# The first layer of a third batch in block form, and q and k loaded in the order that the transposes read

## The chip, the core and the metric

One core of one Trainium2 chip. TensorE multiplies matrices and writes to PSUM. VectorE (DVE in the profile) and ScalarE (ACT) read PSUM and work elementwise. GpSimd (POOL) issues the loads that turn f32 into bf16 on the way, and SyncE (SP) issues the DMA transposes and the stores. The metric is the device time of one execution in microseconds, as a median over runs.

## The reference

```python
# q, k, v: (8, 12, 448, 64)   w_in: (768, 2048)   w_out: (2048, 768), all f32
scores = scale * np.matmul(q, k.transpose(0, 1, 3, 2))
attn = np.maximum(scores, 0.0) ** 2 / S
attn_out = np.matmul(attn, v)
x = attn_out.transpose(0, 2, 1, 3).reshape(B * S, H * D)      # (3584, 768)
h = x @ w_in
g = 0.5 * h * (1.0 + erf(h * inv_sqrt2))
out = g @ w_out                                               # (3584, 768)
```

So each of eight batches has twelve heads of attention with a squared relu in place of the softmax, and all 3584 rows then go through two layers with an exact Gelu between them.

## The kernel before

**Attention.** Heads are taken four at a time (three groups g per batch, G = 3), and the 448 keys in seven steps i of 64. A step (`add_steps`, L610) is four score matmuls on quarters of TensorE's array into one of three two-bank PSUM buffers `w` (L623), then a relu on ScalarE or VectorE (L635, L637), then a square on VectorE (L644). After the seven steps of a group comes AV (`add_av`, L683: 28 matmuls, also into a `w` buffer), and two copies bring its result to `xT`, the transposed x of the batch.

**First layer.** In the plain form (`add_f1`, L730) a batch is 16 chunks m of 128 columns of w_in, each six matmuls of 448 columns, followed by one Gelu on ScalarE (L740). In the block form (`add_blocks`, L811, and `add_block`, L859) w_in and x are each cut into 2 x 2 blocks and multiplied with seven block products p1 to p7 in place of eight; sums of w_in blocks (`add_wsums`, L794), sums of x blocks (`xs`, L837) and five additions per quarter (v2, v3, c22, c21, c12, L904) make up for the eighth. The order of products is p1, p6, p2, p7, p5, p4, p3, each for two halves y; matmuls there have 224 columns (L870). Batches 6 and 7 have this form, and all others the plain one.

**Second layer.** Rows are taken in groups of 256 (`add_group`, L1000), and each group is seven products of eight matmuls of 384 columns (L1036), with four sums on VectorE ahead (L1017) and seven passes out of PSUM (L1070 and copies). Group 0 is made plainly (`add_plain`, L1131). The activations `h_sb` are a ring of two batches.

**Loads.** For batches 3 to 7, `add_load` (L446) issues three DMAs on GpSimd: k into `nk`, q into `nq` and v into `v_sb`. When they have landed, VectorE copies k and q into the tiles `pk` and `pq` in another order of columns (`add_pk`, L466, three copies a batch; `add_pq`, L477, six). SyncE then issues three transposes kT<-pk and four qT<-pq (`add_T_dma`, L569, L578), and a small copy on GpSimd (`add_gate`, L590) waits for those of qT: GpSimd works through its queue in order, so the loads of the next batch stand behind this gate. The first score step of a batch needs all four qT transposes of it. `nq`, `nk`, `pq` and `pk` exist once; qT and kT twice; v three times.

**What sets the order.** A planner in the program (`Scheduler`, L110) places every operation on an engine by estimated times. For the first 270 operations the order is a list written out by hand (`ORDER`). From then on TensorE's order is a list, `pe_q`: each batch b from 2 to 7 has six slots of attention steps, with first-layer chunks and second-layer products from one list `flow` between them, in equal shares per batch; `LEADS` puts some of them ahead of a batch. After attention, the list `end` follows: block batches with four products of a group woven in, and the remaining groups. VectorE and ScalarE choose by deadlines (`deadlines`, L206), which are worked out backwards from when TensorE needs each result. SyncE's transposes are ordered with the stores by the same deadlines. The plan is made twice (`PASSES`), and the last plan is used.

Of the kernel before, what the change touches and what calls it, by code (L numbers as in the profile page):

```python
# [49 lines left out]
PASS_BIAS = -0.4  # L50
SUM_BIAS = -0.3
TSUM_BIAS = 0.2
LEADS = {3: 8}
LAST = 256
PASSES = 2
NEAR = 0.5
QUEUE_STEP = 1.5
LOAD_MARGIN = 2.0


def cols(half):
# [41 lines left out]
class Scheduler:  # L103
# [39 lines left out]
    def pick(self, ops, only=None):  # L143
        top, near = None, []
        for n, op in enumerate(ops):
            t = self.ready(op)
            if t is None:
                continue
            for x, (eng, dur, lat) in enumerate(op.engines):
                if self.late and only not in (None, eng):  # L150
                    continue
                est = max(t, self.free[eng])
                if isinstance(lat, tuple):
                    est = max(est, self.landed[-8])
                if eng == "PE" and op.mode != self.mode:
                    est += SWITCH
                key = (est + op.bias + x * op.other, n)
                if top is None or key < top[0]:
                    top = (key, est, op, eng, dur, lat)
                near.append((est + x * op.other, est, n, op, eng, dur, lat))  # L160
        if top and self.late and only in ("ACT", "DVE"):
            edge = min(near)[0] + NEAR
            top = min(
                ((self.late[id(o)], n), est, o, eng, dur, lat)
                for at, est, n, o, eng, dur, lat in near if at <= edge
            )
        return top
# [26 lines left out]
    def run(self, fixed):  # L194


        for _ in range(PASSES):
            self.reset()
            self.place(fixed)
            self.deadlines()  # L200
        self.open = []
        n = len(ORDER.split())
        for est, op, eng in self.log[:n] + sorted(self.log[n:], key=lambda x: x[0]):
            op.fn(eng)

    def deadlines(self):  # L206


        after = {id(o): [] for o in self.open}
        for o in self.open:  # L210
            for d in o.deps:
                if id(d) in after:
                    after[id(d)].append(o)
                elif isinstance(getattr(d, "op", None), Op):
                    after[id(d.op)].append(o)
        takers = {}
        for _, o, _ in self.log:
            for name in o.need:
                takers.setdefault(name, []).append(o)
        for name, v in self.given.items():  # L220
            n = self.buffers[name]
            for x, o in enumerate(v):
                if x + n < len(takers[name]):
                    for y in [o] + list(o.joint):
                        after[id(y)].append(takers[name][x + n])
        self.late = {}
        t = math.inf
        order = sorted(self.log, key=lambda x: x[0])
        pe = [o for _, o, e in order if e == "PE"]
        ideal, at = {}, 0.0  # L230
        for o in pe:
            ideal[id(o)] = at
            at += o.engines[0][1]
        shift = pe[-1].start - ideal[id(pe[-1])]
        queue = math.inf
        for est, o, e in reversed(order):
            t = ideal[id(o)] + shift if e == "PE" else est + 50.0
            if e == "SP" and o.mode == "X":
                t = min(t, queue - QUEUE_STEP)
            for s in after[id(o)]:  # L240
                if id(s) in self.late:
                    t = min(t, self.late[id(s)] - (o.done - o.start))
            if e == "SP" and o.mode == "X":
                queue = t
            self.late[id(o)] = t
# [38 lines left out]
def kernel(  # L284
# [151 lines left out]
    def add_v(b, g0, g1):  # L436
# [6 lines left out]
        for g in range(g0, g1):  # L443
            ld_v[b, g] = [o]

    def add_load(b, g0=0, g1=G):  # L446
        add_k(b, g0, g1)
        add_q(b, g0, g1)
        add_v(b, g0, g1)
# [219 lines left out]
    def add_av(blk, bias):  # L669
# [31 lines left out]

        def get_x():
            if b not in xT:
                xT[b] = xpool.tile([128, HP, S], BF16, tag="xT", name="xT")
            return xT[b][:, 2 * g : 2 * g + 2, cols(half)]

        old = [o for (bb, *_), o in F1.items() if bb == b - 2]
        xs = X[b, g, half] = []
        for j in range(2):
            xs.append(  # L710
# [54 lines left out]
    def wtile(n, m):  # L765

        if n == 3:
            return wpart(0, 1), m
        if n not in wsum:
            tags = {1: ("nq",), 2: ("pq",), 4: ("nk", "pk")}[n]  # L770
            wsum[n] = [
                natpool.tile([128, K1, FF // 2 // len(tags)], BF16, tag=t, name=f"ws{n}")
                for t in tags
            ]
        k = M1 // len(wsum[n])
        return wsum[n][m // k], m % k
# [7 lines left out]
    def add_wsums(after, done):  # L784

        last = [o for (bb, *_), o in list(Pq.items()) + list(Pk.items()) if bb == B - 1]
        last += [o[0] for (bb, *_), o in list(Tq.items()) + list(Tk.items()) if bb == B - 1]
        add, sub = mybir.AluOpType.add, mybir.AluOpType.subtract

        def one(n, m0, op, a, b, deps):  # L790
            m1 = m0 + M1 // 2
            return sch.add(
                (("DVE", 0.95, 1.07),),
                lambda e: V.tensor_tensor(wcols(n, m0, m1), a(m0, m1), b(m0, m1), op=op),  # L794
                deps + last + after,
            )

        def part(i, j):
            return lambda m0, m1: wpart(i, j, m0, m1)

        def summed(n):
            return lambda m0, m1: wcols(n, m0, m1)

        for m0 in (0, M1 // 2):
            s1 = one(1, m0, add, part(0, 1), part(1, 1), [])
            s2 = one(2, m0, sub, summed(1), part(0, 0), [s1])
            s4 = one(4, m0, sub, part(1, 0), summed(2), [s2])
            s3 = one(3, m0, sub, part(0, 0), part(0, 1), [s1] + done)
            WS[m0] = {1: s1, 2: s2, 3: s3, 4: s4}

    def add_blocks(b):  # L811
# [10 lines left out]
        def t(n):  # L822
            def fn():
                if "t" not in box:
                    tag = {B - 2: "qT", B - 1: "kT"}[b]
                    box["t"] = tpool.tile([128, 4, K1, HS], BF16, tag=tag, name="xs")
                return box["t"][:, n - 1]

            return fn

        gone = old_T(b + 2 if b == B - 2 else b + 1)
        gone = [o for (bb, *_), o in QK.items() if bb == B - 2]

        def xsum(n, op, l, r, deps):
            return sch.add(
# [23 lines left out]
    def add_block(b, m4, y, ms, bank, x, t, TS, xs, old, half):  # L859
# [39 lines left out]
        def passed(name, to, other, deps, need=()):  # L899
            def fn(e):  # L900
                if other is None:
                    copy(e, get(to), ps(name))
                else:
                    V.tensor_add(get(to), ps(name), get(other))  # L904

            eng = e_copy(S, 1)
            return sch.add(eng if other is None else eng[:1], fn, deps, need=need, bias=PASS_BIAS)

        def gelu(src, r, c, deps, frees=()):
            def fn(e):  # L910
# [376 lines left out]
    def at(b, n):  # L1287
        return [at_slot(b, n)]

    add_load(3)  # L1290
    flow, plans = [], {}
    F1B = {2: 1, 3: 2, 4: 3, 5: 4, 6: 5}
    GROUPS = {2: (1,), 3: (2, 3), 4: (4, 5), 5: (6,), 6: (7, 8)}
    for b in range(2, B):
        add_steps(steps(b), dve=True)
        if b == 2:
# [7 lines left out]
        if b + 1 < B:  # L1304

            n = {2: 2, 3: 2}.get(b, 1)
            add_pk(b + 1, 0, G, after=at(b, n) + SUMS[0] + SUMS[1])
            add_pq(b + 1, 0, G, after=at(b, n) + SUMS[0] + SUMS[1])
            add_T_dma(b + 1, [at(b, n + (y >= 4)) for y in range(7)])
            if b + 2 < B:  # L1310
                add_gate(b + 1)
                add_load(b + 2)
        flow += [y for g in GROUPS.get(b, ()) for y in add_group(g)]
    add_wsums(at(B - 1, 1), [F1[B - 3, m, None] for m in range(KF)])

    def woven(x, y, n):


        tx, ty, gone, out = sum(o[0] for o in x), sum(o[0] for o in y[:n]), 0.0, []
        k = 0  # L1320
        for o in x:
            out.append(o)
            gone += o[0]
            while k < n and (k + 0.5) / n < gone / tx:
                out.append(y[k])
                k += 1
        return out + y[k:]

    end = woven(add_blocks(B - 2), add_group(9), 4)
    g10 = add_group(10)  # L1330
    end += g10 + woven(add_blocks(B - 1), add_group(11), 4)
    end += add_group(12) + add_group(13)
    pe_q.extend(x[1] for x in first_atoms)
    share, gone, edge = sum(x[0] for x in flow) / (B - 2), 0.0, 0.0

    def take():
        w, o = flow.pop(0)
# [3 lines left out]
    for b in range(2, B):  # L1341
        for _ in range(LEADS.get(b, 0)):
            gone += take()
        start, edge = gone, edge + share
        for n, slot in enumerate(plan[b]):
            for kind, x in slot:
                if kind == "FFN":
# [37 lines left out]
```

## Time and profile before

| what | value |
|---|---|
| median of 3 runs | 376.32 us (376.17 to 376.45) |
| the profiled execution, own time | 375.98 us |
| its span in the profile | 374.2 us |
| attention of batch 2 starts, attention of batch 7 ends | 65.3 us, 290.2 us |
| score matmuls of batches 3, 4, 5, 6, 7 start | 113.1, 140.1, 177.4, 214.6, 251.5 us |
| last matmul starts | in the group from 368.3 us |

Some groups of instructions, as the page counts them over the whole span: busy time, mean of one, and idle time of the engine just before them.

```profile
L635 ACT ACTIVATE a_sq<-ps 128x896 bf16<-128x896 f32 (+1 forms) x143 | 122.8, 914 | 57.5 <-PE ps L623 57.5
...
L644 DVE TENSOR_TENSOR a_sq<-a_sq 128x896 bf16<-128x896 bf16 (+1 forms) x169 | 98.7, 615 | 11.2 <-ACT a_sq L635 10.1
...
L904 DVE TENSOR_TENSOR part<-pb,part 128x448 f32<-128x448 f32 x40 | 23.1, 618 | 6.3 <-PE pb L870 6.2
...
L590 POOL COPY gate<-qT 128x4 bf16<-128x4 bf16 x5 | 1.3, 266 | 155.6 <-DMA qT<-pq 155.6
```

A line names the source line, the engine, the output and input tiles with their shapes, and the count. In the last one GpSimd sits idle for 155.6 us before the five gates: this is where it waits for the transposes.

### The profile page before, as it was taken

What the parts mean: (1) busy time and instruction counts of PE and PEld (TensorE: products, weight loads), DVE (VectorE), ACT (ScalarE), POOL (GpSimd) and SP (SyncE); (2) the same over time, 40 slices, a digit from 0 to 9 for tenths busy, and PEclk for the clock granted to TensorE, in tenths of its full rate; (3) what the DMA queues carried; (4) which work ended last, traced back from release to release, by engine and by line L of the source; (5) the groups of instructions that cost most, each with busy time, mean ns of one, the idle gap of its engine ahead of it and who ended that gap; (6) DMA issues with size and microseconds to landing.
All of it is one profiled execution on the core that took longest, in us unless ns stands there. A gap on an engine that the chain in (4) does not pass through costs nothing.

```text
span 374.2 us, 8324 instructions
## 1 busy us (share of the span) xinstructions
PE 363.0 (97%) x3485; PEld 215.4 (58%) x3485; DVE 284.3 (76%) x517; ACT 200.9 (54%) x301; POOL 46.0 (12%) x69
## 2 busy tenths in 40 slices
PE   8799999999999999999999999999999999999995
PEld 7566645455554455544555445544555886688663
DVE  3998981799848787985889768946888879785762
ACT  4998864746337865666546575657562333035100
POOL 8666400300002011002000020000000000000000
PEclk9999999999999999999999999999999999999999
DMA  9999999997579969989333799400020201210233
GB/s 175 195 201 204 202 190 114 171 205 143 94 171 162 146 75 190 238 113 159 64 101 79 140 154 181 120 3 0 2 86 12 75 2 31 90 49 2 85 86 84
DMA packets 69685, 42.96 MB, mean 115 GB/s; under 512 B 37776, under 2 KB 66192, under 8 KB 69648
## 3 DMA queue, kind: packets, MB, share of 16 engines
q0 software_dynamic: 30512, 22.47, 40.2%
q1 hardware_dynamic: 38768, 19.46, 25.5%
q8 instruction: 27, 0.44, 0.5%
q10 hardware_dynamic: 368, 0.51, 0.4%
q14 instruction: 10, 0.08, 0.1%
HBM read 45.61 MB, written 11.01 MB: 151 GB/s over the span
## 4 chain that ended last, share of the span: by engine, by line
PE 84%; DVE 6%; ACT 4%; issue 2%; DMA 2%; POOL 1%; DVEq 0%; ACTq 0%; POOLq 0%
PE pso L1036 32%; PE psh L730 29%; PE ps L623 8%; PE pb L870 7%; PE pav L683 4%; ACT a_sq L635 4%; PE pso L1131 3%; DVE a_sq L644 3%; DVE part L904 2%; DMA nk<-in_k_dram 2%; DVE a_sq L637 1%; DVE xT L387 0%; DVE kT L387 0%; PE tp L517 0%; ACT xT L389 0%
## 5 line engine op out<-in xcount | busy, mean ns | idle before, releaser
L635 ACT ACTIVATE a_sq<-ps 128x896 bf16<-128x896 f32 (+1 forms) x143 | 122.8, 914 | 57.5 <-PE ps L623 57.5
L730 PE MATMUL psh<-xT,win_sb 128*128 128x448 bf16 (+1 forms) x612 | 114.2, 342 | 0.1
L644 DVE TENSOR_TENSOR a_sq<-a_sq 128x896 bf16<-128x896 bf16 (+1 forms) x169 | 98.7, 615 | 11.2 <-ACT a_sq L635 10.1
L730 PEld LDWEIGHTS <-win_sb 128*128 128x128 bf16 x612 | 57.4, 98 | 53.7 <-issue 9.2
L740 ACT ACTIVATE h_sb<-psh 128x448 bf16<-128x448 f32 x96 | 52.5, 547 | 34.3 <-PE psh L730 34.0
L1036 PEld LDWEIGHTS <-s_sb 128*128 128x128 bf16 x424 | 40.6, 98 | 27.7 <-issue 2.5
L623 PE MATMUL ps<-qT,kT 64*64 64x448 bf16 (+1 forms) x756 | 48.5, 336 | 3.1 <-ACT a_sq L635 0.7
L637 DVE TENSOR_SCALAR a_sq<-ps 128x896 bf16<-128x896 f32 x26 | 28.2, 1088 | 28.5 <-PE ps L623 28.1
L1036 PEld LDWEIGHTS <-h_sb 128*128 128x128 bf16 x312 | 29.8, 98 | 20.9 <-issue 2.4
L1036 PE MATMUL pso<-wout_sb,h_sb 128*128 128x384 bf16 x208 | 38.1, 326 | 0.0
L1036 PE MATMUL pso<-t_sb,s_sb 128*128 128x384 bf16 x208 | 38.1, 326 | 0.0
L1036 PE MATMUL pso<-wout_sb,s_sb 128*128 128x384 bf16 (+2 forms) x216 | 38.1, 320 | 0.0
L683 PE MATMUL pav<-a_sq,v_sb 64*64 64x448 bf16 (+1 forms) x756 | 36.8, 330 | 0.8 <-ACT a_sq L635 0.4
L623 PEld LDWEIGHTS <-kT 64*64 64x64 bf16 x756 | 18.6, 105 | 26.9 <-issue 21.3
L1070 DVE TENSOR_TENSOR osb<-pso,p_sb 128x384 f32<-128x384 f32 x39 | 21.6, 555 | 9.5 <-PE pso L1036 7.3
L683 PEld LDWEIGHTS <-v_sb 64*64 64x64 bf16 x756 | 21.1, 107 | 13.1 <-issue 2.3
L387 DVE CAST xT<-pav 128x448 bf16<-128x448 f32 (+1 forms) x44 | 24.3, 582 | 5.5 <-PE pav L683 4.9
L904 DVE TENSOR_TENSOR part<-pb,part 128x448 f32<-128x448 f32 x40 | 23.1, 618 | 6.3 <-PE pb L870 6.2
L913 ACT ACTIVATE h_sb<-part 128x448 bf16<-128x448 f32 x24 | 13.3, 577 | 18.4 <-DVE part L904 18.3
L590 POOL COPY gate<-qT 128x4 bf16<-128x4 bf16 x5 | 1.3, 266 | 155.6 <-DMA qT<-pq 155.6
L870 PEld LDWEIGHTS <-win_sb 128*128 128x128 bf16 x192 | 18.4, 98 | 3.2 <-issue 2.1
L1036 PE MATMUL pso<-t_sb,h_sb 128*128 128x384 bf16 x104 | 19.0, 326 | 0.0
(60 smaller groups left out, 262.1 us busy)
## 6 DMA issues: line engine op xcount, KB each, us to landing
nk<-in_k_dram POOLq DMA_DIRECT2D x5, 672.0 KB, 6.7
nq<-in_q_dram POOLq DMA_DIRECT2D x5, 672.0 KB, 9.3
v_sb<-in_v_dram POOLq DMA_DIRECT2D x5, 672.0 KB, 13.4
out_dram<-osb SPq DMA_DIRECT2D x8, 336.0 KB, 3.1
wout_sb<-in_moe_w_out_dram POOLq DMA_DIRECT2D x2, 1152.0 KB, 11.7
v_sb<-in_v_dram POOLq DMA_DIRECT2D x9, 224.0 KB, 9.0
out_dram<-osb SPq DMA_DIRECT2D x7, 288.0 KB, 3.1
out_dram<-osb SPq DMA_DIRECT2D x8, 240.0 KB, 2.8
```

Source lines behind the costliest of these rows:

```text
L387: V.tensor_copy(dst, src)
L623: nc.tensor.matmul(ps[64 * j : 64 * j + 64, e, x * w : x * w + w], kT[r, g, i * 128 + 64 * j : i * 128 + 64 * j + 64], qT[r, 2 * g + j, co ...
L635: A.activation(ar, ps, AF.Relu, scale=c_att)
L637: V.tensor_scalar(ar, ps, c_att, 0.0, op0=mybir.AluOpType.mult, op1=mybir.AluOpType.max,)
L644: V.tensor_mul(box["a2"][:, :, :used], ar, ar)
L683: nc.tensor.matmul(pav[0][o2 : o2 + 64, e, :w], vt[b][r, 2 * g + e, bass.ts(i, D)], box["a2"][r, e, o : o + w], start=(i == 0), stop=(i == ...
L730: nc.tensor.matmul(ph[:, x * n : x * n + n], win_sb[:, kd, bass.ts(m + x, 128)], xT[b][:, kd, c], start=(kd == 0), stop=(kd == KD - 1),)
L740: A.activation(h_ring()[:, m : m + nm, o + c.start : o + c.stop], box[0][:, :S].rearrange("p (x n) -> p x n", x=nm), AF.Gelu,)
L870: nc.tensor.matmul(bank[name][:, y, z * HS : z * HS + HS], w[:, k, bass.ts(mm, 128)], right()[:, k], start=first and k == 0 and z == 0, st ...
L904: V.tensor_add(get(to), ps(name), get(other))
L1036: nc.tensor.matmul(box[bank][:, n0:n1], left()[:, kf], right[:, kf, n0:n1], start=bool(need) and kf == 0, stop=kf == K2 - 1, skip_group_ch ...
L1070: V.tensor_add(out()[:, n0:n1], box[bank][:, n0:n1], other()[:, n0:n1])
```

## The change

Batch 5 (B - 3) takes the block form as well, behind attention: `end` becomes blocks of 5 with group 7, group 8, blocks of 6 with group 9, group 10, blocks of 7 with group 11, and groups 12 and 13. The tiles `xT` of batches 5 to 7 and two of the w_in sums move to pools that are free by then. In the weave, a group's product now stands after the fourth and the tenth of each fourteen block products. The block form's first copy out of PSUM (v1) is made by ScalarE alone.

For batches 3 to 7, k and q are loaded straight into `pk` and `pq` in the permuted order, with runs of 64 elements, by 6 and 12 DMAs; the VectorE copies of these batches go. The planner's deadlines for TensorE now come from its operations one after the other without waits; it makes five plans and takes the one that ends first; and it may ignore the preference for ScalarE where ScalarE would be late.

```diff
-LEADS = {3: 8}
+LEADS = {3: 4}
+SHARES = (1.3, 1.0, 1.0, 1.0, 1.0, 1.0)
-PASSES = 2
+PASSES = 5
+LIMIT = 0.1
+QUEUE_MARGIN = 5.0
+WIDE = 2.0
...
-                near.append((est + x * op.other, est, n, op, eng, dur, lat))
+                other = op.other
+                if x and self.late:
+                    first = max(t, self.free[op.engines[0][0]]) + op.engines[0][2]
+                    if first > self.limit[id(op)] + LIMIT:
+                        other = 0.0
+                near.append((est + x * other, est, n, op, eng, dur, lat))
...
+        best = None
         for _ in range(PASSES):
             self.reset()
             self.place(fixed)
             self.deadlines()
-        self.open = []
+            end = self.free["PE"]
+            if best is None or end < best[0]:
+                best = (end, list(self.log))
+        self.open, self.log = [], best[1]
...
             ideal[id(o)] = at
-            at += o.engines[0][1]
-        shift = pe[-1].start - ideal[id(pe[-1])]
+            at = o.start + o.engines[0][1]
...
-                    t = min(t, self.late[id(s)] - (o.done - o.start))
+                    m = QUEUE_MARGIN if e == "SP" and o.mode == "X" else 0.0
+                    t = min(t, self.late[id(s)] - (o.done - o.start) - m)
+            self.limit[id(o)] = t + (o.done - o.start)
...
+    def add_wide(b):
+        def k_fn(e):
+            def fn():
+                to = get_p()[1].rearrange("p g (i e d) -> e p g i d", e=2, d=D)
+                src = kv_view(k, b, 0, G).rearrange("p (g e) (i d) -> e p g i d", e=2, d=D)
+                for g in range(G):
+                    nc.gpsimd.dma_start(to[e][:, g], src[e][:, g])
+            return fn
+        def q_fn(e, j):
+            def fn():
+                to = get_p()[0].rearrange("p c (g j e d) -> j e g p c d", j=2, e=2, d=D)
+                src = q[b].rearrange("(g e j) (p c) d -> j e g p c d", e=2, j=2, c=NC)
+                for g in range(G):
+                    nc.gpsimd.dma_start(to[j][e][g], src[j][e][g])
+            return fn
...
+        ks = [dma(k_fn(e), WIDE * n / 2, war(b), G) for e in range(2)]
+        qs = [dma(q_fn(e, j), WIDE * n / 4, war(b), G) for e in range(2) for j in range(2)]
...
     def add_load(b, g0=0, g1=G):
+        if b > 2:
+            return add_wide(b)
...
-            tags = {1: ("nq",), 2: ("pq",), 4: ("nk", "pk")}[n]
+            tags = {1: ("nq",), 2: ("pq",), 4: ("xT", "pk")}[n]
...
-            return sch.add(eng if other is None else eng[:1], fn, deps, need=need, bias=PASS_BIAS)
+            return sch.add(eng[1:] if other is None else eng[:1], fn, deps, need=need, bias=PASS_BIAS)
...
-    F1B = {2: 1, 3: 2, 4: 3, 5: 4, 6: 5}
-    GROUPS = {2: (1,), 3: (2, 3), 4: (4, 5), 5: (6,), 6: (7, 8)}
+    F1B = {2: 1, 3: 2, 4: 3, 5: 4}
+    GROUPS = {2: (1,), 3: (2, 3), 4: (4, 5), 5: (6,)}
...
-            add_pk(b + 1, 0, G, after=at(b, n) + SUMS[0] + SUMS[1])
-            add_pq(b + 1, 0, G, after=at(b, n) + SUMS[0] + SUMS[1])
...
+    def woven(x, y):
+        out, y = [], list(y)
+        for n, o in enumerate(x):
             out.append(o)
+            if n % 14 in (3, 9):
+                out.append(y.pop(0))
+        return out + y
+
+    end = woven(add_blocks(B - 3), add_group(7))
+    end += add_group(8)
+    end += woven(add_blocks(B - 2), add_group(9))
     g10 = add_group(10)
-    end += g10 + woven(add_blocks(B - 1), add_group(11), 4)
+    end += g10 + woven(add_blocks(B - 1), add_group(11))
     end += add_group(12) + add_group(13)
...
-        start, edge = gone, edge + share
+        start, edge = gone, edge + total * SHARES[b - 2] / sum(SHARES)
```

## The prediction

> **What bounds the kernel now.** I read the page's busy line and the chain that ended last, then TensorE's row in time order.
>
> ```profile
> span 374.2 us, 8324 instructions
> ...
> PE 363.0 (97%) x3485; PEld 215.4 (58%) x3485; DVE 284.3 (76%) x517; ACT 200.9 (54%) x301; POOL 46.0 (12%) x69
> ...
> PEclk9999999999999999999999999999999999999999
> ...
> PE 84%; DVE 6%; ACT 4%; issue 2%; DMA 2%; POOL 1%; DVEq 0%; ACTq 0%; POOLq 0%
> ```
>
> TensorE is 97% busy at full granted clock and is 84% of the chain. So time leaves this kernel if TensorE gets fewer columns to stream, or if its small gaps close. Busy matmuls overlap, so I price them by the distance between starts:
>
> ```profile
> 103.92 9.24 PE L730 MATMUL psh<-xT,win_sb 128*128 128x448 bf16 x48
> 113.09 0.57 PE L623 MATMUL ps<-qT,kT 64*64 64x448 bf16 x8
> ...
> 154.40 0.87 PE L623 MATMUL ps<-qT,kT 64*64 64x448 bf16 x8
> 155.20 4.71 PE L730 MATMUL psh<-xT,win_sb 128*128 128x448 bf16 x24
> ...
> 166.91 0.55 PE L623 MATMUL ps<-qT,kT 64*64 64x448 bf16 x8
> 167.39 4.71 PE L730 MATMUL psh<-xT,win_sb 128*128 128x448 bf16 x24
> ...
> 296.13 1.31 PE L870 MATMUL pb<-xs,ws 128*128 128x224 bf16 x12
> 297.54 0.73 PE L870 MATMUL pb<-xs,win_sb 128*128 128x224 bf16 x6
> 298.11 1.46 PE L1036 MATMUL pso<-t_sb,s_sb 128*128 128x384 bf16 x8
> 300.09 0.73 PE L870 MATMUL pb<-xs,win_sb 128*128 128x224 bf16 x6 [0.52 <-DVE part L904]
> ```
>
> Columns: start, length, instruction, count, and the wait before it. Three readings follow. The plain first layer costs (113.09 - 103.92 - 0.10 for the switch to attention) / 48 = 0.189 us for a 448-column matmul. In block form twelve 224-column matmuls stand 1.15 us apart elsewhere in this row (329.32, 330.47, 331.62), so 0.0958 us each; eight of 384 columns take 1.30 us. And there are holes: 296.13 + 1.15 = 297.28, but the next starts at 297.54 (0.26); 298.11 + 1.30 = 299.41, but the next starts at 300.09 (0.68). Three more holes of 0.26 follow at 309.12, 333.03 and 343.93: 1.72 us in the two block batches. A further hole is hidden inside attention: two score steps after an AV take 0.80 us (154.40 to 155.20) or 0.48 (166.91 to 167.39). From 65 us on, the long form stands 10 times: 3.2 us in all.
>
> **The arithmetic of TensorE.** Batch 5 loses 16 x 6 = 96 matmuls of 448 columns (96 x 0.189 = 18.16 us) and gains 7 x 8 x 3 = 168 of 224 columns (168 x 0.0958 = 16.10). Nothing else on TensorE changes in number: **-2.06 us**. Adding up both whole sequences by the same prices, with 0.1 us for each change between attention and feed-forward, gives 352.91 and 350.84, the same 2.07; the number of such changes is therefore kept. Up to 65 us both sequences are identical.
>
> **The new weave.** A second-layer product (1.30 us) now stands between p5 and p4 in every half, instead of once inside p4 and elsewhere after p3. The 0.26 before p4 is a wait for VectorE's v3 (p4 overwrites the bank that v3 reads), and 1.30 us covers it; v3's own length is 0.62. The 0.68 was the same engine, behind attention's leftovers at the first block. The copy v1 is now always ScalarE's, which takes six 0.62 us copies off VectorE; it then stands behind Gelus there, but the other p1, two p6 and a second-layer product lie before the p2 that needs it. I take back 1.2 of 1.72; bounds 0 and 1.7. **-1.2 us**.
>
> **VectorE and ScalarE in the shorter attention stage.** From the first score of batch 2 to the first block:
>
> ```profile
> 65.30:290.20 224.90, 223.64 (x1953) 116.26 (x1952) 176.27 (x322) 133.04 (x189) 15.13 (x21) 1.00 0.68 117
> ```
>
> After the length come busy times of TensorE, its weight loads, VectorE (176.3), ScalarE (133.0) and GpSimd. VectorE and ScalarE together are 69% of twice 224.9. The stage loses 18.2 us of first layer and two groups (2 x 7 x 1.30 = 18.2): 188.5 us remain. Work that leaves: 16 Gelus x 0.547 = 8.8; two groups x (4 sums x 0.684 + 7 passes x 0.555) = 13.2; permutes of five batches (30 of 36 of 8.1 us, 15 of 18 of 6.6) = 12.3. So 309.3 - 34.3 = 275 over 377: **73%**. Batch 3 alone (113.1 to 140.1) ran at 78% with no counted stall, so 73% should be carried; without the removed permutes it would be 76%. The planner may now give VectorE a relu whenever ScalarE would be late (26 become 33 in the new order), which aims at the hidden 0.32 us holes. New holes and closed ones: between +4 (all 18 AVs with a hole twice as long: 18 x 0.64 - 3.2 = 8, half of it taken) and -3.2. I take **-0.5**.
>
> In the end stage VectorE has three batches of blocks (20 adds x 0.62 + 4 x 0.5 = 14.4 each) and seven groups (6.6) over 112 us: 80%, a little above the 76% that it shows from 290 to 370 now.
>
> **The loads.** Here the change adds most, off the critical path. Per batch 3 to 7 three load instructions on GpSimd become 19, and the 768 k and 1344 q packets of 896 and 512 bytes become 2 x 5376 of 128 bytes, written where the transposes read. pq and pk are single tiles, so load(b+1) waits (through the gate) for all transposes of b: a closed ring per batch. The trace of before has no 128-byte load. Nearest rows, packets in quiet stretches of 3 us (512 bytes) and 2 us (994 of 256 bytes):
>
> ```profile
> DMA packets 1165, 0.60 MB, mean 199 GB/s; under 512 B 2, under 2 KB 1165, under 8 KB 1165
> ...
> q0 software_dynamic: 1165, 0.60, 145.6%
> ...
> DMA packets 1210, 0.38 MB, mean 188 GB/s; under 512 B 994, under 2 KB 1209, under 8 KB 1209
> ...
> q0 software_dynamic: 1209, 0.36, 169.4%
> ```
>
> 1165 in 3 us on 16 engines is 41 ns per packet; packet records of 896 bytes come at 231 per us, 69 ns. That is a line of 3.5 ns + 0.0735 per byte: 22 ns for 256 bytes, 13 for 128. The second answer: (32,000 - 215 x 41) / 994 = 23 ns, on the line. The Trainium skill ("DMA: Bandwidth & Descriptors", Specifications) speaks against the change: below 512 bytes an engine reads, modifies and writes, so line rate is lost. Taken as a doubling, that is 26 ns. By the row 10,752 x 13 / 16 = 8.7 us for q and k, by the rule 17.5; now it is (768 x 69 + 1344 x 41) / 16 = 6.8. I take the row, since 256 bytes show no doubling. But then GpSimd is slower than the data:
>
> ```profile
> 167.82 0.82 POOL L421 DMA_DIRECT2D nk<-in_k_dram  x1 [0.33 <-issue]
> 168.63 0.95 POOL L336 DMA_DIRECT2D nq<-in_q_dram  x1
> ```
>
> A 768-packet issue takes 0.82 us and a 448-packet one 0.74 (start of the kernel): 6 x 0.83 + 12 x 0.74 = 13.9 us. A second rule, "SBUF — State Buffer" (section "SBUF: two separate sides", its trap about DVE and DMA), says that VectorE's fast modes lock GpSimd out while it writes descriptors. Between 10 and 30 us VectorE is 92 to 94% busy, most of it such operations, and the issues still take 0.63 to 0.77 us; by the rule, half a 0.6 us operation each, 5.4 us more per batch.
>
> So q lands 0.3 + 13.9 + 2 = 16 us after the gate; four qT transposes (1.28 apart, 2.7 to landing) end 6.7 later. Needed by the first score of each batch, taken from the summed sequence plus the offset of before's (10.6 to 13.9 us): batch 3 at 107, 4 at 132, 5 at 163, 6 at 193, 7 at 223. Ready: batch 3 behind the two w_out loads (these end at 79 now) and the first stores, 98; batch 4 has load 98.5 to 115, its slot at 115, kT and qT to 125; batch 5 load to 141, behind group 2's stores, 158; batch 6 181; batch 7 205. Slack 5 to 18 us: **0**. With 26 ns it is still 0, about.
>
> **Sum.** 374.2 - 2.1 - 1.2 - 0.5 = 370.4. The profiled execution took 375.98, 1.8 more than its span, and the median is another 0.3 above it: 370.4 + 2.1 = **372.5 us**.
>
> **Rivals.**
> - *The load ring becomes the bound (slower).* The ring is about 0.3 + 2 + data + 6.7, against 30 us between batches. It decides when q and k need more than 21.5 us, 32 ns per packet. For it: each 512-byte packet record lasts 60 ns, and only their overlap gives 41; the line through the lengths would be 32 ns at 128 bytes if small packets did not overlap, and transposes and v share the engines. Against it: 256 bytes. At 36 ns the ring is 33.5 us: batch 7 is ready at 232.6 instead of 223, +9: **382**. Chance 0.08.
> - *The gain is eaten by new waits* in the denser attention stage (+4) with the holes closed by half: **375.7**. For it, the 93% or so of both engines that batch 7 would need if all w_in sums fell into it; against it, the 73% mean. Chance 0.12.
> - *More holes close than I count*: all 3.2 hidden and 1.7 of the blocks: 374.2 - 2.1 - 4.9 + 2.1 = **369.3**. Chance 0.16.
> - That the block form isn't done is excluded by the order of instructions: 168 block matmuls more, 96 plain ones fewer.
>
> Forecast 0.64, 371 to 374.5. A measurement here tells 0.2% (0.75 us) from no change. Faster: 0.64 + 0.16 + half of 0.12 = 0.86; same 0.04; slower 0.10. Range 369.2 to 376.3.
>
> **What would show it.** pb matmuls 504 in number at 0.096 us; no hole before p4; DVE without pq and pk copies beyond batch 2; load issues of about 14 us per batch and 128-byte packets at 13 to 15 ns; no wait of the score matmuls on qT's transposes. Wrong if ps waits for DMA, if ps waits for relu more than 3 us in all, or if the blocks of batch 5 start later than 256 us.

## The result, and the profile after

The changed kernel takes **371.11 us** as a median of 4 runs (370.77 to 371.97); the kernel before took 376.38 us in the same job (4 runs, 376.17 to 376.46). The ratio is 0.986, with a 95% interval of 0.9846 to 0.9882. The profiled execution took 370.77 us. From its page, first the span, the busy line, the granted clock and the chain that ended last:

```profile
span 368.9 us, 8544 instructions
...
PE 358.9 (97%) x3557; PEld 222.1 (60%) x3557; DVE 288.3 (78%) x493; ACT 200.8 (54%) x308; POOL 108.0 (29%) x149
...
PEclk9999999999999999999999999999999999999999
...
PE 87%; DMA 4%; DVE 4%; ACT 2%; POOL 1%; issue 1%; DVEq 0%; POOLq 0%; ACTq 0%
```

TensorE is still the bound, at full clock. GpSimd's busy time has more than doubled, from 46.0 to 108.0 us, and none of it shows: GpSimd has 1% of the chain. Now the groups that answer to those shown of before, and the new loads (busy time, mean of one, idle time before it):

```profile
L698 ACT ACTIVATE a_sq<-ps 128x896 bf16<-128x896 f32 (+1 forms) x136 | 117.4, 914 | 44.6 <-PE ps L686 44.5
...
L976 DVE TENSOR_TENSOR part<-pb,part 128x448 f32<-128x448 f32 x60 | 34.6, 619 | 18.4 <-PE pb L942 18.4
L476 POOL DMA_DIRECT2D pq<-in_q_dram x60 | 41.8, 704 | 10.1 <-DVE a_sq L707 6.4
```

The block additions are now 60, the squares on VectorE are as many as before (169), and 7 relus have moved from ScalarE (143 to 136) to VectorE. The 60 issues of q are new; the 30 of k take 28.9 us, 0.966 each. In GpSimd's own list of groups the gate shows what became of the ring of loads:

```profile
L653 POOL COPY gate<-qT 128x4 bf16<-128x4 bf16 x5 | 1.2, 245 | 64.4 <-DMA qT<-pq 64.4
```

It was 155.6 us before. Most of GpSimd's idle time at the gates has become time in which it issues loads.

**Where the time came from.** TensorE's row in time order shows the first blocks of batch 5 (start, length, instruction, count):

```profile
257.95 1.31 PE L942 MATMUL pb<-xs,ws 128*128 128x224 bf16 x12
259.10 1.46 PE L1108 MATMUL pso<-t_sb,s_sb 128*128 128x384 bf16 x8
260.40 1.31 PE L942 MATMUL pb<-xs,win_sb 128*128 128x224 bf16 x12
```

The starts are 1.15 us apart after twelve 224-column matmuls (257.95 to 259.10) and 1.30 after eight of 384 (259.10 to 260.40). That is the streaming time, so no hole is left, here or anywhere else in the three block batches. In attention the row looks like this:

```profile
152.42 0.87 PE L686 MATMUL ps<-qT,kT 64*64 64x448 bf16 x8
153.22 1.47 PE L1108 MATMUL pso<-t_sb,s_sb 128*128 128x384 bf16 x8
...
163.16 0.55 PE L686 MATMUL ps<-qT,kT 64*64 64x448 bf16 x8
163.64 3.58 PE L800 MATMUL psh<-xT,win_sb 128*128 128x448 bf16 x18
```

Both pairs of score steps follow an AV. From start to start the first takes 0.80 us and the second 0.48, so the first has a hole of 0.32. I counted such gaps between starts over the whole row in both traces, and all spans below are counted so. Four of after's five holes in attention are of this kind; the fifth, about 0.4 us, is a second-layer product at 98.50 that waits for VectorE (0.34 <-DVE osb in the row). The first score of batch 2 comes at 65.02 us (65.32 before), the first block at 252.04 (290.22), and the last group of matmuls at 362.75 (368.33).

| source | us |
|---|---|
| columns of batch 5: 96 x 0.189 less 168 x 0.0958 | -2.06 |
| holes between block products: 1.72 before, 0 after | -1.72 |
| holes in attention from 65 us on: 10 (3.10 us) before, 5 (1.67) after | -1.43 |
| first score of batch 2 earlier | -0.30 |
| sum; the last group of matmuls came 5.58 earlier | -5.51 |
| from there to the end of the span: 5.87 before, 6.15 after | +0.28 |
| span: 374.2 to 368.9 | -5.3 |

The row of -0.30 is no gain of the change: the nine other traces at full clock up to there have this score at 65.02 to 65.41, whichever part of the change they hold. What the change explains is the first three rows, 5.21 us.

### The profile page after: what moved, and what is told of

Its sections match the earlier page's. It is cut to its first block, busy times and chain, and to the rows that moved or that the text cites. A ratio compares the mean times of both kernels' runs of the same rounds, so it can differ in the third digit from the quotient of the medians.

```text
span 368.9 us, 8544 instructions
## 1 busy us (share of the span) xinstructions
PE 358.9 (97%) x3557; PEld 222.1 (60%) x3557; DVE 288.3 (78%) x493; ACT 200.8 (54%) x308; POOL 108.0 (29%) x149
## 4 chain that ended last, share of the span: by engine, by line
PE 87%; DMA 4%; DVE 4%; ACT 2%; POOL 1%; issue 1%; DVEq 0%; POOLq 0%; ACTq 0%
PE pso L1108 32%; PE psh L800 24%; PE pb L942 13%; PE ps L686 8%; PE pav L746 6%; PE pso L1203 3%; DMA v_sb<-in_v_dram 2%; DVE a_sq L707 2%; DMA nk<-in_k_dram 2%; ACT a_sq L698 2%; POOL nk L434 0%; POOL v_sb L452 0%; POOL nq L349 0%; PE tp L580 0%; DVE a_sq L700 0%
## 5 line engine op out<-in xcount | busy, mean ns | idle before, releaser
L698 ACT ACTIVATE a_sq<-ps 128x896 bf16<-128x896 f32 (+1 forms) x136 | 117.4, 914 | 44.6 <-PE ps L686 44.5
L707 DVE TENSOR_TENSOR a_sq<-a_sq 128x896 bf16<-128x896 bf16 (+1 forms) x169 | 97.5, 617 | 7.5 <-ACT a_sq L698 7.2
L800 PE MATMUL psh<-xT,win_sb 128*128 128x448 bf16 (+1 forms) x516 | 96.6, 340 | 0.1
L810 ACT ACTIVATE h_sb<-psh 128x448 bf16<-128x448 f32 x80 | 43.9, 549 | 24.1 <-PE psh L800 23.9
L700 DVE TENSOR_SCALAR a_sq<-ps 128x896 bf16<-128x896 f32 x33 | 35.9, 1090 | 18.3 <-PE ps L686 17.8
L686 PE MATMUL ps<-qT,kT 64*64 64x448 bf16 (+1 forms) x756 | 47.3, 336 | 2.2 <-ACT qT L402 0.6
L976 DVE TENSOR_TENSOR part<-pb,part 128x448 f32<-128x448 f32 x60 | 34.6, 619 | 18.4 <-PE pb L942 18.4
L476 POOL DMA_DIRECT2D pq<-in_q_dram x60 | 41.8, 704 | 10.1 <-DVE a_sq L707 6.4
L985 ACT ACTIVATE h_sb<-part 128x448 bf16<-128x448 f32 x36 | 19.8, 578 | 19.9 <-DVE part L976 19.8
L467 POOL DMA_DIRECT2D pk<-in_k_dram x30 | 28.9, 966 | 1.5 <-issue 0.9
## 6 DMA issues: line engine op xcount, KB each, us to landing
wout_sb<-in_moe_w_out_dram POOLq DMA_DIRECT2D x2, 1152.0 KB, 12.1
```

What stands on the lines that cost most here:

```text
L467: nc.gpsimd.dma_start(to[e][:, g], src[e][:, g])
L476: nc.gpsimd.dma_start(to[j][e][g], src[j][e][g])
L686: nc.tensor.matmul(ps[64 * j : 64 * j + 64, e, x * w : x * w + w], kT[r, g, i * 128 + 64 * j : i * 128 + 64 * j + 64], qT[r, 2 * g + j, co ...
L698: A.activation(ar, ps, AF.Relu, scale=c_att)
L700: V.tensor_scalar(ar, ps, c_att, 0.0, op0=mybir.AluOpType.mult, op1=mybir.AluOpType.max,)
L707: V.tensor_mul(box["a2"][:, :, :used], ar, ar)
```

## The experiments

All experiments ran in three jobs. The kernel before took 376.08, 376.12 and 376.12 us in them, and each ratio is against that. The names say from which kernel one starts: b_ from before, a_ from after. No kernel leaves any of the computation out. After itself was not run again in these jobs, and its interval is wide (0.9846 to 0.9882, or 1.4 us), so a difference from it of a few tenths tells nothing. Holes are counted in the one profiled execution, which need not be a median one: near 20 us, b_plan and a_two had one stretch of 3.4 us at half the granted clock, and their first score of batch 2 comes at 65.79 and 66.36.

### Parts of the change put alone into the kernel before

**b_weave: only the new order of products.**

```diff
         for n, o in enumerate(x):
             out.append(o)
+            if n % 14 in (3, 9):
+                out.append(y.pop(0))
+        return out + y
...
+    end = woven(add_blocks(B - 2), add_group(9))
```

> The kernel before (376.4) with the new weave alone. Theory of the account: the five holes of the block batches (1.72 us, four of 0.26 in front of p4 and one of 0.68) are waits for VectorE that a second-layer product between p5 and p4 covers: 374.7 to 375.1, and in the trace no hole in front of p4. Rival (the copy v1 on ScalarE or the planner closed them): 376.1 or more, holes of 0.26 still there.

Measured: 374.62 us, ratio 0.9956 (0.9943 to 0.9969). Its TensorE row, at the first blocks of batch 6:

```profile
297.66 1.46 PE L1036 MATMUL pso<-t_sb,s_sb 128*128 128x384 bf16 x8
298.96 1.31 PE L870 MATMUL pb<-xs,win_sb 128*128 128x224 bf16 x12
```

The second-layer product now runs where the kernel before waited, p4 follows it after 1.30 us, and all five holes are gone. The ten holes in attention stay, and one of 0.23 between two second-layer products is new. So the weave alone closes the 1.72 us, without the change of v1.

**b_v1: only the first block copy on ScalarE alone.**

```diff
-            return sch.add(eng if other is None else eng[:1], fn, deps, need=need, bias=PASS_BIAS)
+            return sch.add(eng[1:] if other is None else eng[:1], fn, deps, need=need, bias=PASS_BIAS)
```

> The kernel before with the block form's copy v1 on ScalarE alone. Theory: no change, 376.1 to 376.7, the holes before p4 stay. Rival (v1 on VectorE delays v3 and so makes the holes): 374.7 to 375.2.

Measured: 375.34 us, 0.998 (0.9973 to 0.9988): 0.74 us faster, where no change was expected, and short of the rival's 374.7 to 375.2. In its trace the four holes of 0.26 stay and the one of 0.68 is gone. That execution took 376.06 and gained nothing: attention has two holes more (0.28 and 0.55 us). So v1 was part of what made TensorE wait at the first block; that this hole is the 0.74 of the median fits in size, but no execution without the new holes was profiled. a_v1both below says whether that matters once the weave is there.

**b_plan: only the planner.** The lines of the diff from `LIMIT` to `self.limit`, with `PASSES = 5`, as shown in the change.

> The kernel before with the planner's changes alone (deadlines from the wait-free sequence, five plans, a relu to VectorE where ScalarE would be late, margin for transposes). Theory: closes holes of attention: of ten long forms of the two score steps after an AV (0.32 us each) four to six are left, 374.4 to 375.2. Rival (the relief of VectorE by the loads closes them, not the planner): 376.1 to 376.6 and still eight to ten long forms.

Measured: 375.21 us, 0.9977 (0.9969 to 0.9986). Attention has 7 holes (2.17 us) in place of 10, and a new one of 0.31 between two second-layer products. The 7 left lie between the theory (4 to 6 left) and the rival (8 to 10), and the time at the slow edge of the theory's 374.4 to 375.2: the planner closes holes by itself, but fewer than expected.

**b_wide: only the permuted loads.** `add_wide` is added, and the calls of `add_pk` and `add_pq` for batches 3 to 7 go.

> The kernel before with the permuted loads alone, 19 load instructions per batch for three, no VectorE copies for batches 3 to 7. Theory: VectorE is not what TensorE waits for, so 375.7 to 376.5; the ring of load and transposes (27 us in the changed kernel) is shorter than the 37 us of a batch here, batch 3 with 27 us at the edge. Rival (the 12 us of VectorE copies carry the gain): 373 to 374.5. Third case (the ring stops batch 4): 377 to 380 with score matmuls waiting for qT.

Measured: 375.53 us, 0.9985 (0.9978 to 0.9991), 0.55 us faster, a little better than the 375.7 to 376.5 expected and short of the rival's 373 to 374.5. Attention has 8 holes (2.48). VectorE makes 20 relus there from 65 to 252 us where before has 16: the time that the permutes leave is used for relus.

### Parts of the change taken out of the kernel after

**a_two: batch 5 plain again.** The shares and leads go back with it.

```diff
-LEADS = {3: 4}
-SHARES = (1.3, 1.0, 1.0, 1.0, 1.0, 1.0)
+LEADS = {3: 8}
+SHARES = (1.0, 1.0, 1.0, 1.0, 1.0, 1.0)
...
-    end = woven(add_blocks(B - 3), add_group(7))
-    end += add_group(8)
-    end += woven(add_blocks(B - 2), add_group(9))
+    end = woven(add_blocks(B - 2), add_group(9))
```

> The changed kernel (371.1) with batch 5 back in the plain form inside attention, and its shares and leads as before; loads, planner, weave and v1 as changed. Theory: 2.06 us of columns come back and the holes stay closed: 373.0 to 373.6. Rival (the third block batch carries the gain by more than its columns, since it shortens the attention stage or the other parts only pay with it): 375 or more.

Measured: 372.52 us, 0.9904 (0.9889 to 0.9919): 1.4 us more than after, less than the 2 us expected. Attention has only 2 holes (0.62 us) here, where after has 5 (1.67). The third block batch thus brings 2.06 us of columns and gives about 1.05 back in holes; the difference of the two, 1.0, is within a few tenths of the 1.4 measured. What goes with the holes stands in the stretch from 65 to 252 us: of its 187 us, VectorE and ScalarE are busy 144.3 and 106.0 in a_two (67% of both) and 159.6 and 119.3 in after (75%). What leaves that stage for the end is TensorE's work, so the same relus and squares fall into less time.

**a_oldweave: the weave of before** with three block batches (the reverse of b_weave's edit).

> The changed kernel with the old weave: second-layer products after every quarter of the block products. Theory: about five to six holes of 0.26 us in three block batches come back: 372.3 to 373.2. Rival (v1 on ScalarE or the planner closed them): 371.0 to 371.5.

Measured: 372.54 us, 0.9903 (0.9889 to 0.9916). Its TensorE row:

```profile
258.20 1.31 PE L942 MATMUL pb<-xs,ws 128*128 128x224 bf16 x12
259.61 0.73 PE L942 MATMUL pb<-xs,win_sb 128*128 128x224 bf16 x6
```

258.20 + 1.15 = 259.35, and the next starts at 259.61: the hole of 0.26 before p4 is back. It stands twice in each block batch, six times in all (1.56 us); attention is as in after. The difference in time is 1.43 us.

**a_oldplan: the planner of before** (the reverse of b_plan's edit).

> The changed kernel with the planner of before (two plans, old deadlines, ScalarE preferred for relus always). Theory: with two thirds of the relief of VectorE but no choice of the engine by lateness, the attention stage has seven to ten holes in place of five: 371.7 to 373.0. Rival (the planner only shifts holes and the loads and weave make the gain): 370.9 to 371.4, five or fewer holes.

Measured: 372.04 us, 0.9892 (0.9879 to 0.9906). Attention has 8 holes (2.50 us) where after has 5, and TensorE pauses 0.64 us before the first scores of batch 5, at 162.22: the gate behind that batch's qT stands at 162.33 here and at 157.24 in after, so the planner's margin for SyncE's queue counts too. The planner's part is 0.9 us in this kernel by the medians (1.5 between the two profiled executions), as it was in b_plan (0.9).

**a_v1both: v1 on either engine**, as before the change.

```diff
-            return sch.add(eng[1:] if other is None else eng[:1], fn, deps, need=need, bias=PASS_BIAS)
+            return sch.add(eng if other is None else eng[:1], fn, deps, need=need, bias=PASS_BIAS)
```

> The changed kernel with the block form's copy v1 on either engine again. Theory: the weave covers the block stage alone, so no hole comes back: 370.8 to 371.6. Rival (v1 on ScalarE is needed since VectorE is 80% busy in the end stage): holes before p4 or p3 and 372 or more.

Measured: 370.83 us (370.52 to 370.92), 0.9857 (0.9842 to 0.9872). The holes are those of after. The interval holds after's ratio, so this is no difference that can be told. VectorE makes eight of the twelve v1 copies here, so v1 on ScalarE alone is worth nothing that can be told beside the weave.

### Costs put on, to size what was taken as free

**a_copies: VectorE work like the removed permutes, but off the path of the loads.** Nine copies of parts of v onto themselves per batch, between the load of v and AV; 45 in all, as many as the removed ones.

```diff
+            for g in range(G):
+                ld, todo = ld_v[b, g], [(slice(0, 128), 0, 896), (slice(0, 112), 0, 512), (slice(0, 112), 384, 896)]
+                for p, c0, c1 in todo:
+
+                    def again(e, g=g, p=p, c0=c0, c1=c1):
+                        x = vt[b].rearrange("p h f -> p (h f)")[p, 896 * g + c0 : 896 * g + c1]
+                        V.tensor_copy(x, x)
...
+                    ld = [sch.add((("DVE", d, d + 0.12),), again, list(ld))]
+                ld_v[b, g] = ld
```

> The changed kernel with the removed VectorE copies put back as copies of v in place (three of 896 and six of 512 elements wide per batch 3 to 7 in sum about the same VectorE time), off the ring of load and transposes. Theory: both engines go from 73% to 76% of the attention stage, which costs 0 to 1.0 us in new holes: 371.1 to 372.1. Rival (VectorE's relief is what lets the shorter stage run without waits): 374 or more.

Measured: 373.26 us, 0.9931 (0.9918 to 0.9943): 2.15 us more than after, between what the theory and the rival expected. Attention has 12 holes (3.96 us). VectorE's groups from 65 to 252 us show the copies (busy time, mean of one, idle time before it):

```profile
L516 DVE COPY v_sb<-v_sb 112x512 bf16<-112x512 bf16 (+1 forms) x45 | 16.7, 379 | 0.6
```

In the same list VectorE makes 13 relus, where after has 23:

```profile
L712 DVE TENSOR_SCALAR a_sq<-ps 128x896 bf16<-128x896 f32 x13 | 14.1, 1088 | 14.9 <-PE ps L698 14.8
```

```profile
L700 DVE TENSOR_SCALAR a_sq<-ps 128x896 bf16<-128x896 f32 x23 | 25.1, 1091 | 17.8 <-PE ps L686 17.7
```

What that does is seen at one AV, the first of batch 4. In after it starts at 131.88, and each engine makes one relu beside it, in the rows of ScalarE and VectorE:

```profile
131.91 0.92 ACT L698 ACTIVATE a_sq<-ps 128x896 bf16<-128x896 f32 x1 [1.02 <-PE ps L686]
```

```profile
132.10 1.09 DVE L700 TENSOR_SCALAR a_sq<-ps 128x896 bf16<-128x896 f32 x1
```

Both are done by 133.2, when the AV ends, and the next two score steps (133.20) take 0.48 us. In a_copies the same AV starts at 132.47. VectorE has a copy out of PSUM at 132.18 and a copy of v at 132.65, and ScalarE makes the relus one after the other:

```profile
132.50 3.43 ACT L710 ACTIVATE a_sq<-ps 128x896 bf16<-128x896 f32 x4 [0.77 <-PE ps L698]
```

The first two of these end at about 132.50 + 3.43 / 2 = 134.2. The two score steps that start at 133.80 take 0.80 us there: the second has to wait for a `w` buffer until its relu is through. The same pattern stands at the hole of after that was shown above: four relus in a row on ScalarE from 151.13, while VectorE works for a group. So a hole of 0.32 comes where VectorE does not take one of the two relus beside an AV. This holds beyond the examples: the traces of all kernels but a_q24 have 192 AVs from 65 us on that two score steps follow. At 83 of them ScalarE makes both relus, and each of these pairs takes 0.80 to 0.92 us. At 109 each engine makes one, and 108 of these pairs take 0.48 to 0.57; the one exception (1.05, in b_v1) has VectorE's relu begin 0.92 us into the AV, behind the copies of q into `pq`.

The copies took longer than the removed permutes, which took 12.1 us from 65 to 252 in before:

```profile
L477 DVE COPY pq<-nq 112x512 bf16<-112x512 bf16 x30 | 6.7, 284 | 0.4 <-DMA nq<-in_q_dram 0.4
...
L466 DVE COPY pk<-nk 128x896 bf16<-128x896 bf16 x15 | 5.4, 384 | 1.5 <-DMA nk<-in_k_dram 1.5
```

The reason is that these copies, unlike the permutes of before, run while GpSimd issues loads. Nine of the 45, all begun during an issue, took 0.38 to 0.78 us where others of their length took 0.29 or 0.39, and eight of the nine end 0.09 us after that issue does. One such pair of a_copies:

```profile
102.95 0.96 POOL L467 DMA_DIRECT2D pk<-in_k_dram  x1
...
103.39 0.62 DVE L516 COPY v_sb<-v_sb 112x512 bf16<-112x512 bf16 x1
```

Some 2.6 of the 17 us of the copies (45 x 0.379) are this waiting, so the test loads VectorE more than the permutes did. In proportion to busy time, the permutes would cost 2.15 x 12.1 / 16.7 = 1.6 us here (an estimate). In the kernel before, without the third block batch, the permuted loads brought 0.55.

**a_q24: q of a batch in 24 issues in place of 12.** The same packets and bytes.

```diff
                 for g in range(G):
-                    nc.gpsimd.dma_start(to[j][e][g], src[j][e][g])
+                    for c in (slice(0, HC), slice(HC, NC)):
+                        nc.gpsimd.dma_start(to[j][e][g][:, c], src[j][e][g][:, c])
```

> The changed kernel with q in 24 load instructions per batch in place of 12, with the same bytes and packets: GpSimd issues 12 x about 0.62 = 7.4 us longer per batch. The prediction put 5 to 18 us of slack on the ring: by it, 371 to 375. From the trace of the changed kernel the slack is 2.5 to 7 us and the ring 27 us of 30: the ring becomes 34 us and decides, about 4 to 5 us per batch over four to five batches less the first slack: 385 to 398, with score matmuls waiting for qT's transposes.

Measured: 392.39 us as the median of three executions (390.8 to 395.14; a fourth took 397.3), 1.0443 (1.0399 to 1.0486). The table of TensorE's waits has a new first line (total, times, longest):

```profile
PE ps L687 <- DMA qT<-pq: 14.6, 5, 8.5
```

GpSimd's queue shows what is late, in after for the load of batch 6 and in a_q24 for that of batch 5:

```profile
157.24 0.19 POOL L653 COPY gate<-qT 128x4 bf16<-128x4 bf16 x1 [11.45 <-DMA qT<-pq]
...
163.47 8.35 POOL L476 DMA_DIRECT2D pq<-in_q_dram  x12
...
183.49 0.19 POOL L653 COPY gate<-qT 128x4 bf16<-128x4 bf16 x1 [10.82 <-DMA qT<-pq]
```

```profile
140.62 0.19 POOL L654 COPY gate<-qT 128x4 bf16<-128x4 bf16 x1 [9.30 <-DMA qT<-pq]
...
146.91 15.67 POOL L477 DMA_DIRECT2D pq<-in_q_dram  x24
...
174.61 0.18 POOL L654 COPY gate<-qT 128x4 bf16<-128x4 bf16 x1 [11.20 <-DMA qT<-pq]
```

The 24 issues take 7.3 us longer than the 12 with the same data, and the ring from gate to gate takes 34.0 us; in after it takes 26.3 in the turn shown and 28.3 in that of the same batch (128.93 to 157.24). An issue of half the packets is hardly shorter (0.65 us against 0.70). So it is the number of issues, not of packets or bytes, that makes the ring longer here. In after it takes 26 to 28 us against some 30 between the scores of two batches from batch 4 on, which leaves room for two to four microseconds per batch, not for 7. The lateness also adds up from one turn of the ring to the next (the gate of batch 3 is 6.1 us later than in after, that of batch 4 11.7), which the expectation that was worked out from the prediction's slack left out. So this run shows what sets the ring, not how large the slack was; that is read from after's own gates below. Where the rest of the loss comes from is told in the last section.

**a_copyact: p_sb and osb copies of the groups on ScalarE alone**, to free VectorE further.

```diff
-                eng if other is None else eng[:1], fn, deps, need=need, frees=frees,
+                eng[1:] if other is None else eng[:1], fn, deps, need=need, frees=frees,
```

> A step beyond the change: the copies out of PSUM of the second layer's groups go to ScalarE alone (about 19 of 0.56 us leave VectorE, some 8 of them in the attention stage). Putting 12.3 us of copies back on VectorE cost 2.2 us; taking 4.5 us off should close one to three of the five holes left: 370.2 to 370.9. Rival (the copies then stand behind relus and Gelus on ScalarE and hold a PSUM bank that TensorE needs): 371.5 or more, with waits of the second layer's matmuls.

Measured: 371.21 us (370.98 to 372.72), 0.9882 (0.9864 to 0.99). No gain, where 370.2 to 370.9 was expected: attention again has 5 holes (1.55 us), not fewer. The one behind VectorE's osb is gone, and one of the relu kind is new. VectorE makes 24 relus from 65 to 252 us here, against 23 in after: the time freed by these copies was not used for more relus. And in the profiled execution, which took 372.48 (the five took 370.98 to 371.21 or 372.48 and 372.72), TensorE stood still before the first scores of batch 7 (the chunks ahead of them, 18 matmuls from 217.93, were through at 221.5):

```profile
223.07 0.57 PE L686 MATMUL ps<-qT,kT 64*64 64x448 bf16 x8 [1.57 <-issue]
```

The gate of batch 6 stands at 189.80 here, 6.3 us later than in after, and the last qT transpose of batch 7 is issued at 219.38 and takes 1.43. The row names no releaser; that these scores waited for that transpose is read from the order of times.

## Why the prediction was right, point by point

The forecast was 372.5 us, 1.4 above the median. At 371.11 the kernel stands just inside the forecast's own band (371 to 374.5), 1.8 from the rival with all holes closed (369.3). The mechanism and the sign were right; the terms for the holes were too small.

- **Columns, -2.06.** The trace has 504 block matmuls, and twelve of them stand 1.15 us apart, so the price held. a_two measured the whole step at 1.4, with the holes that it brings.
- **Weave, -1.2 of 1.72.** The whole 1.72 went (b_weave: -1.46 by the medians, five holes closed; a_oldweave: six holes back, +1.43). Right in cause. The 0.5 held back was not needed. The argument that ScalarE's v1 stays harmless behind Gelus held; the copies that this takes off VectorE are worth nothing that can be told here (a_v1both).
- **Attention's holes, -0.5.** This was the largest miss: -1.43. It is the net of three parts of the change that the prediction put into one number between +4 and -3.2: the planner (-0.9 in both directions, b_plan and a_oldplan), the relief of VectorE (-0.55 alone in before, 2.15 for more copies in after), and the denser stage (a_two: +1.05 of holes). The parts do not simply add up.
- **"73% should be carried; without the removed permutes it would be 76%."** The sizes were near: 75% in after, and 78% in a_copies (VectorE 164.2 and ScalarE 126.1 of 187 us). What failed is the inference that the three points cost nothing because 78% ran without a counted stall in one batch: two of the ten hidden holes (123.64 and 131.94 us) lie in just that batch. They cost some 2 us (2.15, or 1.6 in proportion). A mean share below one says little about holes of 0.32 us, which arise where VectorE is taken at the moment of an AV and both relus fall to ScalarE.
- **Packets, 13 ns against 26 by the rule ("DMA: Bandwidth & Descriptors").** A stretch of one microsecond of after, when only the new loads ran (packets in it):

```profile
DMA packets 1226, 0.15 MB, mean 154 GB/s; under 512 B 1226, under 2 KB 1226, under 8 KB 1226
```

  1226 on 16 engines is 13.1 ns each. The line drawn through 256, 512 and 896 bytes holds at 128, and the doubling that the rule was read as does not appear in this case.
- **Issues, 13.9 us per batch.** 5.78 + 8.35 = 14.1. Of the two parts, k's issue was longer than its row (0.97 against 0.83) and q's shorter (0.70 against 0.74), so that the sum came out partly by cancelling. The second rule was not tested by the issues from 10 to 30 us: VectorE's operations there are squares, which have two inputs, and operations that read PSUM, not copies within SBUF. Squares take 0.62 us in after whether an issue runs or not. VectorE's copies within SBUF do collide, as a_copies shows: mostly the copy waits for the issue, and four k issues are 0.08 to 0.28 us longer. In after no copy of k or q is left to collide from batch 3 on, and no extra half operation is seen.
- **Slack 5 to 18 us: 0 cost.** The cost was right, the slack was not. The gates stand at 101.7, 128.9, 157.2 and 183.5 us (98, 125, 158 and 181 in the prediction), and the scores of batches 3 to 6 start at 107.2, 131.5, 161.4 and 190.7. That leaves 5.5, 2.5, 4.2 and 7.2 us, where 9, 7, 5 and 12 were expected. One term that was too small is the landing of q, put at 2 us behind its issue. The page of after has 5.0 as the median:

```profile
pq<-in_q_dram POOLq DMA_DIRECT2D x60, 56.0 KB, 5.0
```

  That no score waited was therefore a narrow thing. Batch 7 was to be ready at 205; its last qT transpose is issued at 213.4, behind two output stores in SyncE's queue, and its scores start at 221.3.

Of the rivals, the ring as the bound did not come true, but lies close (its own sum is 33.2 us and +8, not 33.5 and +9): its point of decision was given in nanoseconds per packet, and a_q24 shows that the count of issues reaches it with the packets unchanged. The gain eaten by new waits is excluded for the sum, although a_two shows the waits in it. "More holes close" (369.3) was near in kind: all of the blocks' holes closed, and about half of attention's.

**What was to show it.** No hole before p4, no permutes after batch 2, 14 us of issues, 13 ns, no wait of the scores on qT, and from 65 us on four holes of 0.32 behind relus, 1.3 us against the 3 that were named as the limit: all seen. The blocks of batch 5 start at 252 us, before the 256 named as the limit.

## What to carry to other kernels

When the engine that bounds a kernel is 97% busy, look for its small holes by the distance between starts in its row and give each the instruction that ends it: a product of other work put in front of the waiting one closed 1.7 us here, nearly as much as the arithmetic saved. A mean share of 75% on the engines that feed it is no proof of slack: VectorE copies of 16.7 us in 187 cost 2.15 us here, because they left it no time for the second relu beside an AV. If loads are cut into more DMAs, count the issues on their queue before the bytes, and compare the ring's turn with the time between two batches, since lateness adds up.

## What the hardware showed that was not expected

The waits in a_q24 add up to 14.3 us (8.46, 1.00, 2.83 and 2.04 before batches 4 to 7 in TensorE's row), but its span is 21.6 us longer than after's. The rest is TensorE's clock. Here is TensorE's row about the third wait, and then two stretches of half a microsecond, with the granted clock as the third number from the end (before it stand the busy times of the five engines):

```profile
206.68 0.57 PE L687 MATMUL ps<-qT,kT 64*64 64x448 bf16 x8 [2.83 <-DMA qT<-pq]
```

```profile
208.00:208.50 0.50, 0.50 (x15) 0.37 (x8) 0.39 (x1) 0.03 (x1) 0.50 (x2) 0.50 0.00 0
...
211.50:212.00 0.50, 0.50 (x5) 0.30 (x4) 0.00 (x0) 0.00 (x0) 0.50 (x1) 1.00 2.05 131
```

The clock is 1.00 until 208.0 and half from there, 1.3 us after TensorE has begun to work again, and stays there for 3.4 us; the next score pair starts at 208.74 and what follows it at 209.69, 0.95 us in place of the 0.48 to be had. The same comes after the wait of 2.04 us (half from 242.13 to 245.55), and after the one of 8.46 us, where it starts during the wait, at 136.32, and lasts until 146.56, 6.0 us into the work. After the wait of 1.00 us it stays at 1.00. Half of 3.4 + 3.4 + 6.0 us is 6.4 us lost, which with the waits makes 20.7 of the 21.6. So a stall of 2 us of TensorE cost nearly 4 here.

The changes of the clock lie on a grid. From 136.32 to 146.56, 208.00, 211.41, 242.13 and 245.55 it is 3, 18, 1, 9 and 1 times 3.413 us, and in every other trace of this case too the changes are whole multiples of it apart. This points to the idle time of TensorE within one period of the grid as what decides. Here are two periods of a_q24 and two of a_copyact; the first number after the comma is TensorE's busy time.

```profile
204.59:208.00 3.41, 1.32 (x28) 1.03 (x32) 0.70 (x1) 0.89 (x1) 0.96 (x2) 1.00 0.44 91
208.00:211.41 3.41, 3.41 (x29) 1.61 (x19) 2.08 (x4) 1.75 (x3) 3.41 (x5) 0.50 1.05 67
```

```profile
220.49:223.90 3.41, 1.84 (x26) 0.97 (x28) 0.83 (x2) 1.17 (x3) 0.00 (x0) 1.00 0.56 111
223.90:227.30 3.40, 3.40 (x43) 1.92 (x36) 3.17 (x6) 3.05 (x5) 0.00 (x0) 1.00 0.02 5
```

A period with 2.1 us of idle time is followed by one at half clock (2.0 in the one before 242.13), and one with 1.6 is not. The wait of 1.00 us is split by the grid at 173.87. The Trainium skill ("TensorE: Matmul & The Clock Gate", Part 1) has the clock halved after an idle window of about 3.4 us and restored after a busy one. The length of the window agrees; but it need not be wholly idle. The exact limit stays open: near 20 us, where TensorE's work is in short pieces, the clock of b_plan and a_two fell after periods with 1.2 us of idle time, and that of before did not.
